# An attention and MLP kernel: the first MLP layer of tiles 2 to 8 as seven products of quarter matrices, with sums of weights kept in DRAM

## The chip, the cores and the metric

The kernel runs on one core of a Trainium2 chip. The metric is the device time of one execution in microseconds (us). Beside three plain runs there is one profiled execution, from which all durations of single instructions come.

The engines of a core work at the same time and each takes its instructions in the order of the program. TensorE (PE) multiplies matrices; the profile shows its weight loads apart, as PEld. VectorE (DVE) and ScalarE (ACT) do elementwise work. GpSimd (POOL) takes maxima across partitions. SyncE (SP) starts the transfers between DRAM and the on-chip memory. PE writes its sums into PSUM, eight banks of 128 partitions by 512 floats.

## What is computed

The reference is linear attention with random features, followed by a layer norm and a two-layer MLP with a residual:

```
phi(x)  = exp(h - max(h)) / sqrt(m),   h = x @ omega.T - |x|^2 / 2
attn    = (phi(q) @ (phi(k).T @ v)) / (phi(q) @ sum(phi(k)) + 1e-6)
xn      = (x - mean) / sqrt(var + 1e-6) * g_ln       # x is attn, heads side by side
out     = x + max(xn @ w_ch1, 0) @ w_ch2
```

There are 8 batches of 576 tokens, so 4608 tokens, 8 heads of 64, a width of 512 and a hidden width of 2048. All data are float32.

## The kernel before, in words

The tokens are cut into nine tiles of 512 (t = 0 to 8). For the MLP the hidden width is cut into 16 blocks of 128 (f = 0 to 15). The first layer (`mm1`) makes one block of the hidden layer for one tile: over the four pieces k of the width it multiplies a 128x128 piece of w1 by 512 tokens of the transposed, normalised input `xnT`. Each number is split in a high and a low part in the format fp32r, and three products replace one: high by high, low weights by high, high weights by low. So a block is 12 matmuls of 512 columns into one PSUM bank. `relu` then makes the hidden block: ACT writes the high part (L816), DVE the low part (L818). The second layer (`mm2`) multiplies the four token pieces of the hidden block by a block of w2, again 12 matmuls of 512 columns, into four banks that collect over all f. After the last f, `result` adds x (L849) and sends the tile out. `gen_mlp` puts `mm1` of a block ahead of `mm2` of the block before it, so that PE always has a second-layer block to do while the hidden block is made. All these matmuls are issued by one helper, `rounded`, and so have one line, L786.

The banks are shared out by hand: two for attention and transposes (`b_at`), two for the first layer (`b_h`), four for the second (`b_acc`).

The weights come in as 64-bit numbers and are turned into floats and split on chip (`gen_w`, L343 to L387), mainly on DVE, during tile 0 and into tile 1. All weights then stay on chip: a tile of 512 KB for each of the 16 blocks of w1 and of w2, high and low part side by side.

Attention for later tiles runs between the MLP's products: projections of keys (L514) and queries, exponentials on ACT (L451, L617), maxima of the queries on POOL (L611) which DVE subtracts (L614), sums over keys (L483), the products of queries with them (L681), division and layer norm on DVE. `gen_xnT` normalises (L757), PE transposes (L771), ACT copies the high part (L775), DVE makes the low part (L777).

The order on all engines is made when the program is built. A planner (`Plan`) runs all parts as small generators that ask for a place in memory, wait for a named event, or ask for an engine and a length. It keeps a simulated clock for each engine and always issues the part that can start first and has the lowest rank. The MLP has the highest rank number and so fills what attention leaves of PE; evacuations such as `relu` have rank MOST_URGENT. The lengths that the planner uses are written in the code, for example 0.225 us for one matmul of 512 columns, and the order is fixed by them: on the chip each engine keeps that order, whatever the real lengths are.

Of the kernel before, what the change touches and what calls it, by code (L numbers as in the profile page):

```python
# [12 lines left out]
F32 = mybir.dt.float32  # L13
# [9 lines left out]
P = 128  # L23
# [167 lines left out]
def favor_ffn(ctx, tc, kT, kTr, vF, vR, qT, qD, omT, gT, w1, w2, out):  # L191
# [17 lines left out]
    ps = ctx.enter_context(tc.tile_pool(name="ps", bufs=1, space=PSUM))  # L209
    plan = Plan()  # L210
# [54 lines left out]
    banks = names("b", 8)  # L265
    b_at, b_h, b_acc = banks[0:2], banks[2:4], banks[4:8]
# [71 lines left out]
    def gen_w(n, f):  # L338
# [35 lines left out]
        w = wparts[n, f] = tile_of(tag, [P, 2, DM], F32R)  # L374
        if n == 1:
            g = g_sb[:, f % NK : f % NK + 1]
            scaled(eng, w[:, 0], f32(t), g)
            yield dve(DM)
            nc.vector.scalar_tensor_tensor(  # L379
                out=w[:, 1], in0=f32(t), scalar=g, in1=f32(w[:, 0]), op0=ALU.mult, op1=ALU.subtract  # L380
            )
        else:
            copy(eng, w[:, 0], f32(t))
            yield dve(DM)
            nc.vector.tensor_tensor(out=w[:, 1], in0=f32(t), in1=f32(w[:, 0]), op=ALU.subtract)  # L385
        free(wt, w_turn, load_turn)
        done(("w", n, f))  # L387

# [358 lines left out]
    def gen_xnT():  # L747
        for c in range(NC):
            t, i = divmod(c, TC)
# [8 lines left out]
            done(("xn", c))  # L758
            if i == 0:
                t_t = yield "get", n_xnT  # L760
                xnTs[t] = t_t, tile_of(t_t, [P, 2, NK, T], F32R)
            plan.add(plan.cur.rank, gen_xnT1(t, i, xn, t_n, xn_turn))

# [27 lines left out]
    def mm1(t, f):  # L791
        for k in range(NK):
            yield wait("w", 1, f // NK * NK + k)
        for i in range(TC):
            yield wait("xnT", t, i)
        if not mlp_on:
            mlp_on.append(True)
        t_x, xnT = xnTs[t]
        t_b = yield "get", b_h
        ph = bank(t_b)  # L800
        for k in range(NK):
            yield us(PE, 3 * 0.225)
            w = wparts[1, f // NK * NK + k]
            cs = slice(f % NK * P, (f % NK + 1) * P)
            rounded(ph, w[:, 0, cs], xnT[:, 0, k], start=(k == 0), stop=False)
            rounded(ph, w[:, 1, cs], xnT[:, 0, k], start=False, stop=False)
            rounded(ph, w[:, 0, cs], xnT[:, 1, k], start=False, stop=(k == NK - 1))
        if f == NF - 1:
            free(t_x)
        plan.add(MOST_URGENT, relu(t, f, t_b, ph))  # L810
# [13 lines left out]

    accs = {}

    def mm2(t, f):
        yield wait("w", 2, f)
        yield wait("hid", t, f)
        t_h, hl = hid[t, f]  # L830
# [12 lines left out]
        free(t_h)  # L843

# [20 lines left out]
    def gen_mlp():  # L865
        last = None
        for t in range(NT):
            for f in range(NF):
                if f == 0 and last:
                    yield from mm2(*last)  # L870
                    last = None
# [16 lines left out]
    for f in range(NF):  # L888
        plan.add(RW + RS * (2 * f - 7 if f >= NK else f - NK), gen_w(1, f))
        plan.add(RW + RS * 2 * f, gen_w(2, f))  # L890
    plan.add(RK, gen_keys())
# [17 lines left out]
LATE = 1.0  # L909
WARM, COLD = 0.0, 5.0  # L910
# [47 lines left out]
```

## Time and profile before

| what | value |
| --- | --- |
| median of three runs | 1005.11 us (1004.85 to 1005.9) |
| profiled execution | 1004.26 us |
| its span, first to last instruction | 1002.5 us |
| granted TensorE clock over the span | 1.00 |
| PE busy | 994.9 us (99%) |
| weight loads (PEld) | 814.1 us (81%) |
| DVE busy | 500.5 us (50%) |
| ACT busy | 342.4 us (34%) |
| POOL busy | 136.7 us (14%) |
| read from DRAM, written | 52.64 MB, 9.44 MB |

How to read the profile. A row of a group has the line in the kernel, the engine, the operation, what it writes and reads (`out<-in`, numbers of buffers left out), the shape, the count, the busy time, the mean length of one in nanoseconds, and the idle time of the engine ahead of them with what ended it. A row of the timeline has the start, the length of a run of like instructions, and what they are. Matmuls are pipelined: a matmul's record reaches past the start of the next one, so the time that one costs is read from start to start, not from its length. The last addition of x (L849) of each tile begins at 168.8, 293.1, 408.8, 515.6, 626.6, 725.5, 824.4, 914.7 and 998.8 us. The lengths of the tiles differ because attention work is done between the MLP's products of the earlier ones.

### The profile page before, as it was taken

The page shows a single profiled execution, that of the slowest core. Times are in us where ns is not written, and L with a number is a line of the kernel's source. Part 1 is how long each engine was busy: PE and PEld are TensorE (multiplying, and loading weights), DVE is VectorE, ACT ScalarE, POOL GpSimd, SP SyncE. Part 2 cuts the span into 40 slices and gives each one's busy share as a digit, 9 for nine tenths or more (in the row PEclk, how much of TensorE's full clock was granted, in tenths as well). Part 3 has the DMA queues.
Part 4 walks back from the last instruction along what each step waited for, and adds up shares of the span by engine and source line. Part 5 has one row for each costly group of instructions (what it writes and reads, how often), then busy time and mean ns, then how long its engine had stood idle before and what let it go on. Part 6 is the DMA issues. An engine that isn't in the chain of part 4 may idle for free.

```text
span 1002.5 us, 16490 instructions
## 1 busy us (share of the span) xinstructions
PE 994.9 (99%) x6794; PEld 814.1 (81%) x6794; DVE 500.5 (50%) x1054; ACT 342.4 (34%) x785; POOL 136.7 (14%) x80
## 2 busy tenths in 40 slices
PE   9999999999999999999999999999999999999998
PEld 7887787788778788887888788888888888888887
DVE  6999997375357631673157423751374134113112
ACT  7587755235334520353125321331132111111100
POOL 6000633023001300140005000220032000000000
PEclk9999999999999999999999999999999999999999
DMA  9534332222132100320032100300030010001001
GB/s 355 205 148 176 110 96 84 76 74 65 43 117 77 40 12 1 129 84 1 1 127 65 43 1 11 117 1 1 26 101 1 1 43 1 0 1 43 1 1 43
DMA packets 29740, 63.16 MB, mean 63 GB/s; under 512 B 3424, under 2 KB 3552, under 8 KB 29664
## 3 DMA queue, kind: packets, MB, share of 16 engines
q1 hardware_dynamic: 29664, 62.09, 18.2%
q8 instruction: 54, 0.88, 0.4%
q14 instruction: 22, 0.18, 0.1%
HBM read 52.64 MB, written 9.44 MB: 62 GB/s over the span
## 4 chain that ended last, share of the span: by engine, by line
PE 88%; DVE 8%; issue 1%; DMA 1%; ACT 1%; SPq 0%; DVEq 0%; ACTq 0%
PE b L786 77%; PE b L681 3%; PE b L514 3%; PE b L483 3%; PE b L771 2%; DVE wide L368 1%; DVE w L354 1%; DVE w L379 1%; DVE mb L445 1%; DMA w<-w 1%; DVE hid L818 1%; DVE wide L614 1%; DMA w<-vF 1%; DVE w L385 0%; DVE x L849 0%
## 5 line engine op out<-in xcount | busy, mean ns | idle before, releaser
L786 PE MATMUL b<-w,hid 128*128 128x512 f32 x1728 | 430.1, 391 | 0.0
L786 PE MATMUL b<-xnT,w 128*128 128x512 f32 x1728 | 426.6, 390 | 0.1
L786 PEld LDWEIGHTS b<-xnT,w 128*128 128x128 f32 x1728 | 320.6, 188 | 64.9 <-issue 0.7
L786 PEld LDWEIGHTS b<-w,hid 128*128 128x128 f32 x1728 | 319.2, 188 | 63.6 <-issue 0.7
L818 DVE SCALAR_TENSOR_TENSOR hid<-b,hid 128x512 fp32r<-128x512 f32 x144 | 99.5, 691 | 376.2 <-ACT hid L816 375.8
L816 ACT ACTIVATE hid<-b 128x512 fp32r<-128x512 f32 x144 | 86.6, 601 | 449.4 <-PE b L786 448.9
L611 POOL PARTITION_ALL_REDUCE wide<-wide x72 | 135.6, 1921 | 627.1 <-ACT wide L230 538.5
L451 ACT ACTIVATE kp<-b,mb 128x128 f32<-128x128 f32 x272 | 74.4, 387 | 60.1 <-DVE mb L445 59.9
L614 DVE TENSOR_TENSOR wide<-wide,wide 128x512 f32<-128x512 f32 x72 | 65.6, 916 | 10.3 <-POOL wide L611 9.8
L445 DVE TENSOR_REDUCE mb<-b 128x4 f32<-128x512 f32 x72 | 46.7, 684 | 33.7 <-PE b L514 33.7
L617 ACT ACTIVATE wide<-wide 128x512 f32<-128x512 f32 x72 | 45.3, 635 | 48.5 <-DVE wide L614 47.8
L681 PEld LDWEIGHTS b<-kv,wide 128*64 128x64 f32 (+1 forms) x1088 | 40.5, 140 | 11.6 <-issue 8.6
L582 DVE TENSOR_TENSOR wide<-wide,wide 64x512 fp32r<-64x512 f32 x56 | 44.7, 804 | 8.3 <-ACT wide L580 6.9
L230 ACT COPY wide<-b 128x512 f32<-128x512 f32 x60 | 34.1, 591 | 35.5 <-PE b L786 28.6
L681 PE MATMUL b<-kv,wide 128*64 128x65 f32 (+1 forms) x1088 | 45.1, 227 | 0.0
L483 PEld LDWEIGHTS b<-v,kp 128*64 128x64 f32 (+2 forms) x1120 | 34.0, 138 | 13.5 <-issue 9.5
L483 PE MATMUL b<-v,kp 128*64 128x65 f32 (+2 forms) x1120 | 39.5, 226 | 0.7 <-DVE xnT L777 0.7
L514 PEld LDWEIGHTS b<-om,wide 64*128 64x128 f32 x512 | 31.1, 187 | 11.2 <-issue 7.8
L499 DVE TENSOR_TENSOR kv<-b,kv 128x260 f32<-128x260 f32 x56 | 23.2, 425 | 30.3 <-PE b L483 29.6
L514 PE MATMUL b<-om,wide 64*128 64x128 f32 x512 | 37.2, 285 | 0.0
L580 ACT CAST wide<-wide 128x512 fp32r<-128x512 f32 x56 | 33.4, 624 | 0.0
L696 DVE TENSOR_TENSOR x<-b,st 128x256 f32<-128x256 f32 x72 | 28.5, 418 | 0.4
(62 smaller groups left out, 511.1 us busy)
## 6 DMA issues: line engine op xcount, KB each, us to landing
w<-w SPq DMA_DIRECT2D x32, 512.0 KB, 7.5
wide<-qD SPq DMA_DIRECT2D x56, 256.0 KB, 2.8
out<-x SPq DMA_DIRECT2D x36, 256.0 KB, 2.0
v<-vF SPq DMA_DIRECT2D x28, 260.0 KB, 3.5
wide<-kT SPq DMA_DIRECT2D x28, 256.0 KB, 3.1
wide<-qT SPq DMA_DIRECT2D x8, 256.0 KB, 4.4
w<-vF SPq DMA_DIRECT2D x4, 260.0 KB, 4.7
v<-vR SPq DMA_DIRECT2D x4, 260.0 KB, 3.4
```

Of the source, the lines that this page charges most:

```text
L445: nc.vector.tensor_reduce(out=mb[:, 4 * s : 4 * s + 4], in_=pk, axis=AX.X, op=ALU.max, negate=True)
L451: nc.scalar.activation(out=kp[:, j], in_=pk[:, i], func=AF.Exp, scale=1.0, bias=mb[:, j : j + 1])
L483: nc.tensor.matmul(pv[s, n][m, i], kp[r, slot(h), m], v[r, h], start=(n > 0 or c + i == 0), stop=(n > 0 or (c == NFULL and i == 3)),)
L514: nc.tensor.matmul(pk[h][:, p], kraw[a, p], om[a], start=True, stop=True)
L582: nc.vector.tensor_tensor(out=qs[D:P], in0=qraw[D:P], in1=f32(qs[D:P]), op=ALU.subtract)
L611: nc.gpsimd.partition_all_reduce(mx, qc, P, bass_isa.ReduceOp.max)
L614: nc.vector.tensor_tensor(out=qc, in0=qc, in1=mx, op=ALU.subtract)
L617: nc.scalar.activation(out=qc, in_=qc, func=AF.Exp)
L681: nc.tensor.matmul(pn[a:z, i], phi(blk, h, slice(cols + a, cols + z)), kvs[b][1][:, h], start=True, stop=True)
L786: nc.tensor.matmul(out.rearrange("p (c a b) -> p c a b", a=AW, b=BW), lhsT, rhs.rearrange("p (a c b) -> p c a b", a=AW, b=BW), start=start ...
L816: nc.scalar.activation(out=hl[:, 0], in_=ph, func=AF.Relu)
L818: nc.vector.scalar_tensor_tensor(out=hl[:, 1], in0=ph, scalar=0.0, in1=f32(hl[:, 0]), op0=ALU.max, op1=ALU.subtract)
```

## The change

From tile 2 on (SEVEN = 2) the first layer goes by Strassen's scheme in Winograd's form. The 16 blocks are taken as four groups g of 512 hidden columns. A group of w1 and the tile's input are each cut in four quarters: the width in two halves of 256, the hidden columns in two halves of 256, the tokens in two halves of 256. Instead of eight products of quarters there are seven. Their operands on the side of the input are the quarters B11, B21, B22 and the differences T1 = B12 - B11, T2 = B22 - T1, T3 = B22 - B12, N4 = B21 - T2. On the side of the weights they are three quarters as they are and four sums of quarters.

The sums of weights are made once, on DVE and ACT, while tiles 0 and 1 run (`gen_sides`, `halved`, `lesser`), split in high and low parts, and written to DRAM (`side`, 2 MB for each group). For each tile and group they are loaded again, 512 KB each, into one place on chip for each of the four (`gen_ring`); a place is loaded again when both steps of the group have read it. The four places are those of four w1 blocks, freed by moving one needed half elsewhere (`gen_move`).

Twelve of the 16 blocks of w2 no longer stay on chip either. They are written to DRAM when they are made (`gen_leave`, `kept`) and, from tile 2 on, loaded for each tile, two taking turns in one place (`gen_return`). The six places gained hold operands (three), the differences before they are split (two) and a working tile u (one). The other four operands take the place of `xnT`.

For each tile the operands are made thus: the two token pieces of a pair are transposed and copied whole (`gen_turned`), DVE makes the differences, and each of the seven is split by a copy (ACT or DVE) and a subtraction on DVE (`parted`). The second pair waits until the first has been split.

The first layer is now eight steps a tile, each for two hidden blocks, h of group g (`seven`). A step has seven products of 6 matmuls with 256 columns. The two banks of the first layer hold four halves x, y, v, z of 256 columns:

```
before = (t, g, h - 1) if h else (t, g - 1, 1) if g else (t - 1, NK - 1, 1)
before = before if before[0] >= SEVEN else None
yield wait("moved", g)
yield "get", ("one",)
yield from run(x, 0, plain(0, 0), "B11", True)
yield from run(y, 2, None, "T2")
plan.add(MOST_URGENT, second(t, g, h, before, x, y, u))
yield "get", ("two",)
yield from run(v, 1, None, "T1", True)
yield from run(z, 3, None, "T3")
plan.add(MOST_URGENT, fourth(t, g, h, before, v, z, u))
yield wait("u2", t, g, h)
yield from run(x, 0, plain(0, 1), "B21")
plan.add(MOST_URGENT, first(t, g, h, x, u))
yield from between()
yield wait("c22", t, g, h)
yield from run(v, 4, None, "B22")
yield from run(z, 0, plain(1, 1), "N4")
plan.add(MOST_URGENT, third(t, g, h, before, two, u))
```

`between` is one second-layer block, and another follows each step. `second` copies x to u on ACT and adds y on DVE; `fourth` adds v and z on DVE; `first` makes the half of a hidden block that x holds; `third` adds u to the second bank and makes the rest. All additions have one line, L1104; the matmuls of 256 columns have L1041, those of 512 columns L991 (L786 before), the halves of hidden blocks L1130, the additions of x L1193 (L849 before), the subtraction of the query maxima L717 (L614 before).

The core of the diff; the functions above and the loading and storing are left out:

```
         if n == 1:
+            w = wparts[n, f] = tile_of(tag, [P, 2, 2, HC], F32R)
...
+        if n == 2 and f in LENT:
+            plan.add(LEAVE, gen_leave(f, w))
...
+    def product(out, left, right, start):
+        def passes(x):
+            return x.rearrange("p (a c b) -> p c a b", b=8, c=4)
+
+        for k in range(2):
+            for l, r in ((0, 0), (1, 0), (0, 1)):
+                nc.tensor.matmul(
+                    passes(out), left(k, l), passes(right[:, r, k]), start=start and k + l + r == 0,
+                    stop=k + r == 2, skip_group_check=True,
+                )
...
+    def second(t, g, h, before, x, y, u):
+        if before:
+            yield wait("cc", *before)
+            yield wait("c22", *before)
+        yield act(HC)
+        nc.scalar.copy(out=u[:, 0], in_=x)
+        yield dve(HC)
+        add(u[:, 0], y, u[:, 0])
+        done(("u2", t, g, h))
...
     def gen_mlp():
...
         for t in range(NT):
-            for f in range(NF):
-                if f == 0 and last:
-                    yield from mm2(*last)
-                    last = None
-                yield from mm1(t, f)
-                if last:
-                    yield from mm2(*last)
-                last = t, f
-        yield from mm2(*last)
+            for f in range(NF if t < SEVEN else NF // 2):
+                if f == 0:
+                    yield from one()
+                    yield from one()
+                if t < SEVEN:
+                    yield from mm1(t, f)
+                    yield from one()
+                    last.append((t, f))
+                else:
+                    g, h = divmod(f, 2)
+                    yield from seven(t, g, h, one)
+                    yield from one()
+                    last += [(t, NK * g + h), (t, NK * g + 2 + h)]
...
+SEVEN, HC = 2, DM // 2
+SHARED, HOSTS = (4, 5, 6, 7, 2, 3), 8
+LENT = (*SHARED, *(f + HOSTS for f in SHARED))
+LEAVE, RSIDE = 24, 24
```

At the seam between two tiles PE has three second-layer blocks of the old tile behind the last step's products, and the first step of a tile has none inside it.

More of the change, by code (lines that the diff above doesn't have):

```diff
@@ new lines, in halved, with lesser @@
+    def halved(g, k, n, t_h, t_s, s):
+        hi = tile_of(t_h, [P, 2, HC], F32R)
+        eng = yield "run", {ACT: 0.56, DVE: 0.34}
+        copy(eng, hi, s)
+        yield dma(P * DM)
+        nc.sync.dma_start(sides[g, 0][:, 2 * n : 2 * n + 2, 0, k], f32(hi))
+        plan.add(plan.cur.rank, lesser(g, k, n, t_s, s, hi, t_h))
+    def lesser(g, k, n, t_s, s, hi, t_h):
+        yield dve(DM)
+        nc.vector.tensor_tensor(out=s.bitcast(F32R), in0=s, in1=f32(hi), op=ALU.subtract)
+        free(t_h)
+        yield dma(P * DM)
+        nc.sync.dma_start(sides[g, 0][:, 2 * n : 2 * n + 2, 1, k], s)
+        free(t_s)
+        done(("side", g, n, k))
@@ L764, in gen_xnT1, with parted @@
+    def parted(t, name, i, x):
+        yield wait("op", t, name)
+        o = ops[t, name][1]
+        eng = yield "run", {ACT: 0.3, DVE: 0.28}
+        copy(eng, o[:, 0, :, i * P : (i + 1) * P], x)
+        yield dve(HC)
+        nc.vector.tensor_tensor(
+            out=o[:, 1, :, i * P : (i + 1) * P], in0=x, in1=f32(o[:, 0, :, i * P : (i + 1) * P]), op=ALU.subtract
+        )
+        done(("x2", t, name, i))
     def gen_xnT1(t, i, xn, t_n, xn_turn):
@@ new lines, in add, with fourth @@
+    def add(out, left, right):
+        nc.vector.tensor_tensor(out=out, in0=left, in1=right, op=ALU.add)
+    def second(t, g, h, before, x, y, u):
[4 more added lines that the diff above has]
+        nc.scalar.copy(out=u[:, 0], in_=x)
+        yield dve(HC)
+        add(u[:, 0], y, u[:, 0])
+        done(("u2", t, g, h))
+    def fourth(t, g, h, before, v, z, u):
+        if before:
+            yield wait("hid", before[0], NK * before[1] + 2 + before[2])
+        yield wait("u2", t, g, h)
+        yield dve(HC)
+        add(u[:, 3], v, u[:, 0])
+        yield dve(HC)
+        add(u[:, 3], z, u[:, 3])
+        done(("c22", t, g, h))
@@ new lines, in halves, with first @@
+    def halves(hl, cols, x):
+        yield act(x.shape[1], 1, 0.05)
+        nc.scalar.activation(out=hl[:, 0, cols], in_=x, func=AF.Relu)
+        yield dve(x.shape[1])
+        nc.vector.scalar_tensor_tensor(
+            out=hl[:, 1, cols], in0=x, scalar=0.0, in1=f32(hl[:, 0, cols]), op0=ALU.max, op1=ALU.subtract
+        )
+    def first(t, g, h, x, u):
+        f = NK * g + h
+        t_h = yield "get", n_hid
+        hl = tile_of(t_h, [P, 2, T], F32R)
+        hid[t, f] = t_h, hl
+        yield from halves(hl, slice(0, HC), x)
+        free("one")
+        yield wait("cc", t, g, h)
+        yield from halves(hl, slice(HC, T), u[:, 1])
+        done(("hid", t, f))
@@ new lines, in third @@
+    def third(t, g, h, before, two, u):
+        f = NK * g + 2 + h
+        if before:
+            yield wait("hid", before[0], NK * before[1] + before[2])
+            yield wait("hid", before[0], NK * before[1] + 2 + before[2])
+        yield dve(2 * HC)
+        add(
+            u[:, 1:3], two.rearrange("p (a b) -> p a b", b=HC),
+            u[:, 0:1].to_broadcast([P, 2, HC]),
+        )
+        free("two")
+        done(("cc", t, g, h))
+        yield wait("c22", t, g, h)
+        t_h = yield "get", n_hid
+        hl = tile_of(t_h, [P, 2, T], F32R)
+        hid[t, f] = t_h, hl
+        yield from halves(hl, slice(0, T), u[:, 2:4].rearrange("p a b -> p (a b)"))
+        done(("hid", t, f))
@@ L829, in mm2 @@
         yield wait("hid", t, f)
+        lent = f in LENT
+        if lent and t >= SEVEN:
+            yield wait("back", t, f)
         t_h, hl = hid[t, f]
@@ L843, in mm2 @@
         free(t_h)
+        if lent and t >= SEVEN - 1:
+            free(*n_w[2, f + HOSTS if t >= SEVEN and f in SHARED else f])
     def result(t, i, acc):
```

214 lines of the change are left out of this document (206 added, 8 removed).

## The prediction

> **What bounds the kernel now.** I read the page's busy rows first, then the chain that ended last, then the stages tile by tile, then single stretches of the timeline.
>
> ```profile
> span 1002.5 us, 16490 instructions
> PE 994.9 (99%) x6794; PEld 814.1 (81%) x6794; DVE 500.5 (50%) x1054; ACT 342.4 (34%) x785; POOL 136.7 (14%) x80
> PE 88%; DVE 8%; issue 1%; DMA 1%; ACT 1%; SPq 0%; DVEq 0%; ACTq 0%
> PE b L786 77%; PE b L681 3%; PE b L514 3%; PE b L483 3%; PE b L771 2%; DVE wide L368 1%; DVE w L354 1%; DVE w L379 1%; DVE mb L445 1%; DMA w<-w 1%; DVE hid L818 1%; DVE wide L614 1%; DMA w<-vF 1%; DVE w L385 0%; DVE x L849 0%
> ```
>
> TensorE sets the end, and 77% of the chain is the two MLP layers (L786). DVE is busy half the time, PE almost never waits. So a change is worth what it takes out of PE's stream, less every wait that it puts into it. The stages, cut where the last result (L849) begins, of tiles 1, 2, 5 and 8 (columns: window, length, then busy time and count of PE, PEld, DVE, ACT, POOL, the granted clock, DMA share and GB/s):
>
> ```profile
> 168.80:293.10 124.30, 124.10 (x1099) 99.58 (x1097) 63.24 (x145) 49.88 (x144) 15.02 (x8) 1.00 0.23 67
> 293.10:408.80 115.70, 114.72 (x887) 92.89 (x888) 54.77 (x119) 37.64 (x92) 14.70 (x8) 1.00 0.16 49
> 626.60:725.50 98.90, 98.90 (x546) 80.76 (x545) 42.90 (x90) 24.50 (x46) 14.81 (x8) 1.00 0.10 33
> 914.70:998.80 84.10, 84.04 (x382) 71.28 (x381) 13.78 (x22) 9.56 (x16) 0.00 (x0) 1.00 0.03 12
> ```
>
> Now the pitch of a product of 512 columns, from groups of twelve in the timeline: first two groups of tile 5, then two of tile 7.
>
> ```profile
> 703.88 2.94 PE L786 MATMUL b<-xnT,w 128*128 128x512 f32 x12
> 706.65 2.93 PE L786 MATMUL b<-w,hid 128*128 128x512 f32 x12
> ...
> 862.11 2.80 PE L786 MATMUL b<-xnT,w 128*128 128x512 f32 x12
> 864.75 2.80 PE L786 MATMUL b<-w,hid 128*128 128x512 f32 x12
> ```
>
> Start to start it is 2.77/12 = 0.2308 us in one place and 2.64/12 = 0.220 us in the other, at the same granted clock of 1.00 (the rows above). The kernel has both paces, and a stretch keeps its pace until PE is interrupted. I take their mean, 0.2255, for tiles 2 to 8.
>
> **Part 1: fewer columns streamed (gain).** Seven of nine tiles change. Each had 16 x 12 = 192 first-layer products of 512 columns; it now has 8 steps x 7 quarter products x 6 matmuls = 336 of 256 columns. Taken out: 7 x 192 x 0.2255 = 303.1 us. Put in: 2352 matmuls whose pitch no row shows, since no fp32r product of 256 columns runs today. The nearest rows are a bf16 product of 256 columns, and fp32 products of 65 columns whose 128x128 weights are the longer part:
>
> ```profile
> 37.99 4.09 PE L308 MATMUL b<-spin 128*128 128x256 bf16 x36
> 30.45 0.53 PEld L681 LDWEIGHTS b<-kv,wide 128*128 128x128 f32 x4
> L681 PEld LDWEIGHTS b<-kv,wide 128*128 128x128 f32 x64 | 8.1, 192 | 0.1
> L786 PEld LDWEIGHTS b<-xnT,w 128*128 128x128 f32 x1728 | 320.6, 188 | 64.9 <-issue 0.7 <-DVE xnT L777 0.5
> ```
>
> The bf16 row gives (4.09 - 0.27 for the last one's length)/35 = 0.109 us. In the second row four loads of 0.192 us stand within 0.53 us, so they begin (0.53 - 0.192)/3 = 0.113 us apart: a load's recorded time is not its pitch, and loads overlap each other as well as products. Stream (0.109) and load (0.113) of a 256-column product are then nearly equal. Low bound: the load's pitch, 0.112. High bound: the slow pace keeps its whole extra per product, 0.2308 - 2 x 0.109 + 0.109 = 0.122. I take 0.116, a little nearer to the load row, because both paces occur. Then 2352 x 0.116 = 272.8 us and the gain is 30.3 us; the bounds give 303.1 - 263.4 = 39.7 and 303.1 - 286.9 = 16.2 us.
>
> By the Trainium skill (TensorE: Matmul & The Clock Gate, section Back-to-back issue gap) 256 columns take 262 cycles at 2.4 GHz, 0.109 us, and 512 columns 518, 0.216 us; by that 1344 x 0.216 - 2352 x 0.109 = an estimated 34 us would be saved. The bf16 row agrees, the 512-column rows are 2 to 7% above it, so the rows decide.
>
> **Part 2: waits inside a step (loss).** The order on PE in tile 8, before: the end of a second-layer block and a whole first-layer block (w are weights, hid the hidden layer, xnT the input, b a PSUM bank):
>
> ```order
> L786 MATMUL b_8386<-w_130_1557,hid_8711 128x512 x3
> L786 MATMUL b_8754<-xnT_8272,w_120_1214 128x512 x3
> L786 MATMUL b_8754<-xnT_8272,w_130_1304 128x512 x3
> L786 MATMUL b_8754<-xnT_8272,w_140_1377 128x512 x3
> L786 MATMUL b_8754<-xnT_8272,w_150_1450 128x512 x3
> ```
>
> And in the changed kernel one step (bank b_3454 holds the halves x and y, b_3455 the halves v and z; weights w_50, w_10, w_90, w_130 are the loaded sums):
>
> ```order
> L1041 MATMUL b_3454<-w_40_2540,w_80_970 128x4x8x8 x6
> L1041 MATMUL b_3454<-w_50_2641,w_50_10484 128x4x8x8 x6
> L1041 MATMUL b_3455<-w_60_2738,w_10_10493 128x4x8x8 x6
> L1041 MATMUL b_3455<-xnT_3341,w_90_10502 128x4x8x8 x6
> L1041 MATMUL b_3454<-xnT_3341,w_100_1191 128x4x8x8 x3
> L1041 MATMUL b_3454<-xnT_3341,w_110_1273 128x4x8x8 x3
> L991 MATMUL b_10330<-w_130_10207,hid_10517 128x512 x3
> ```
>
> Before, a first-layer block filled one bank and nothing read it until a second-layer block had run. Now the fifth product adds into x, which ACT must first have copied and DVE must have added to y; only the third and fourth products, 12 x 0.116 = 1.39 us, lie between. What the chain y -> ACT -> DVE -> PE costs, from these rows:
>
> ```profile
> 731.55 0.86 PE L786 MATMUL b<-w,hid 128*128 128x512 f32 x3
> 731.75 0.60 ACT L816 ACTIVATE hid<-b 128x512 fp32r<-128x512 f32 x1 [3.44 <-PE b L786]
> 732.38 0.69 DVE L818 SCALAR_TENSOR_TENSOR hid<-b,hid 128x512 fp32r<-128x512 f32 x1 [0.71 <-ACT hid L816]
> ...
> L230 ACT COPY kv<-b 128x260 f32<-128x260 f32 x16 | 5.6, 376 | 9.9 <-PE b L483 9.7
> L499 DVE TENSOR_TENSOR kv<-b,kv 128x260 f32<-128x260 f32 x56 | 23.2, 425 | 30.3 <-PE b L483 29.6
> L614 DVE TENSOR_TENSOR wide<-wide,wide 128x512 f32<-128x512 f32 x72 | 65.6, 916 | 10.3 <-POOL wide L611 9.8
> ```
>
> ACT starts 0.20 us after the stream has gone on to the next product, and DVE 0.03 us after ACT. So the chain is 0.20 + 0.38 + 0.03 + 0.43 + 0.03 = 1.07 us, 0.32 us inside its cover, if ACT and DVE are free. When DVE is in the middle of something else the cover is gone. The order on DVE in tile 5, before:
>
> ```order
> L818 SCALAR_TENSOR_TENSOR hid_6511<-b_6481,hid_6511 128x512
> L716 BN_AGGR st_5492<-st_5492 128x2
> L582 TENSOR_TENSOR wide_6496<-wide_6487,wide_6496 64x512
> L727 TENSOR_SCALAR st_5492<-st_5492 128x2
> L614 TENSOR_TENSOR wide_6505<-wide_6505,wide_6513 128x512
> ```
>
> and after (L1104 are a step's additions, L717 is what was L614, the query maxima subtracted):
>
> ```order
> L685 TENSOR_TENSOR wide_7794<-wide_7785,wide_7794 64x512
> L1104 TENSOR_TENSOR w_70_3456<-b_3454,w_70_3456 128x256
> L717 TENSOR_TENSOR wide_7813<-wide_7813,wide_7823 128x512
> L1104 TENSOR_TENSOR w_70_3456<-b_3455,w_70_3456 128x256
> L717 TENSOR_TENSOR wide_7820<-wide_7820,wide_7831 128x512
> L1104 TENSOR_TENSOR w_70_3456<-b_3455,w_70_3456 128x256
> ```
>
> Attention's work now stands between additions that PE waits for. DVE's load per tile: a step has 3 additions of 256 (0.42), one of 512 (0.69), two half relus (0.43) and a whole one (0.69), 3.5 us, 28 per tile against 16 x 0.69 = 11 before; the operands add 8 differences and 14 low parts of 0.42 less the four old low parts of 0.69, some 6.5 us. That is +24 us: about 79 of 110 us in tile 2, 67 of 94 in tile 5, 31 of 80 in tile 8. Between 0 (the chain always inside its cover) and 0.92 us a step (always one L614 in front) I take 0.2 us for the 40 steps of tiles 2 to 6, where a mean DVE instruction is 500.5/1054 = 0.47 us and meets a 0.32 us cover, and 0.05 for the other 16: 9 us. The waits on the second pair of banks have the second-layer block of 2.7 us as cover, and cost nothing until DVE is 1.5 us late.
>
> **Part 3: the seams (loss).** The seven operands of a tile (quarters of xn and their differences) replace those of the tile before when its last step has read them; 28 pieces are copied (ACT or DVE) and reduced (DVE) while three second-layer blocks, 8.1 us, run. The first operand needs a copy and a difference of the last one, transposes, an ACT copy, a copy and a difference, about 4 us by the durations above; T2 and T1 follow 2 to 3 us later. I take 0.5 us for each of six seams, 3 us (0 to 10). Into tile 2 only two blocks (5.4 us) cover the same, with four operands left to do first: 3 us (0 to 6).
>
> **Part 4: sums of weights and DRAM.** Making the sums is 8 x (4 of 0.73, 4 of 0.42) = 37 us of DVE and ACT, in tile 1: DVE goes from 63 to about 100 of 124 us. PE has other work there; 1 us (0 to 5). Transfers: each changed tile loads 16 sums and 12 second-layer blocks of 512 KB, 14.7 MB, some 155 GB/s on top of the 12 to 49 in the rows above.
>
> ```profile
> GB/s 355 205 148 176 110 96 84 76 74 65 43 117 77 40 12 1 129 84 1 1 127 65 43 1 11 117 1 1 26 101 1 1 43 1 0 1 43 1 1 43
> w<-w SPq DMA_DIRECT2D x32, 512.0 KB, 7.5
> ```
>
> The first slice shows 355 GB/s, so the sum fits. A ring place is free from its product in one step to the same product in the next: 42 x 0.116 + 24 x 0.2255 = 10.3 us, and a block landed in 7.5 us at the busiest time. So I cost it at nothing; SP issues in order, and if it falls behind, PE waits at every change of group.
>
> **The sum.** -30.3 + 9 + 3 + 3 + 1 = -14.3 us. The profiled run took 1004.26 us (1.8 us around its span); the median of the three runs is 1005.11. So 1005.1 - 14.3, say 990.8 us.
>
> **The rivals.**
> Waits stay small and the pitch is the load's (chance 0.20): -39.7 + 7 or so, about 972 us. For it: PE is busy 99% today though hundreds of attention products wait for DVE and ACT. Against it: those had slack, and the slow pace occurs.
> DVE takes PE's place in tiles 2 to 6 (0.17): each of 40 steps waits for one L614-like instruction, 40 x 0.92 = 37, 0.8 for the others, 7 for the seams: -30.3 + 45 = +15, 1020 us. It decides from (30.3 - 8)/40 = 0.56 us a step. For it: the DVE order above. Against it: DVE is below 75%.
> Loads bind (0.03): each load takes its recorded 0.188 us and the products wait for it, 2352 x 0.188 - 303.1 = +139, 1144 us; it decides from a pitch of 303.1/2352 = 0.129. Against it stands the row of four loads in 0.53 us. Two places of the Trainium skill speak for it. TensorE: Matmul & The Clock Gate, section The mechanism, lets a load overlap products in flight only when it goes to another row group, and here all use all rows. Perfetto Trace Analysis, section Identifying the Most-Contended Engine, judges PE's headroom by the busy share of loads, 81% here, which 1008 more would fill. The trace disagrees with both as far as it shows: 0.188 us loads lie inside 0.220 us products.
> The ring is late (0.06): a kept block goes ahead of a sum on SP's queue and each of 21 changes of group inside a tile waits 2 us, +42 - 14, about 1033 us.
>
> **Chances.** The forecast has 0.54 (some 980 to 1002). About 0.2% (2 us) is what a measurement here can tell from no change. Faster by more: 0.54 + 0.20, less 0.02 for the forecast's upper edge: 0.72. Within 0.2%: that 0.02 and 0.04 of the DVE case: 0.06. Slower: 0.13 + 0.06 + 0.03 = 0.22. Range: 969 (gain of 39.7 with some 4 us of waits) to 1012 (gain of 16.2 with 0.3 us a step and the seams at their bounds, or the milder half of the DVE case); it leaves out loads, ring and the worse DVE cases, some 0.16, and 0.04 below.
>
> **What would show it.** Right: twelve L1041 matmuls start to start 1.35 to 1.47 us; tile 8, where attention is gone, shorter by 192 x 0.220 - 336 x 0.116 = 3.3 us, or a little more at 0.112; PE's waits named L1041 <- DVE, 5 to 15 us in all, mostly in tiles 2 to 6; DVE near 79 us in tile 2. Wrong: a pitch over 0.129; waits over 25 us; PE waiting for DMA at L1041; tile 1 longer than 124 us by more than 5.

## The result and the profile after

| what | before | after |
| --- | --- | --- |
| median, us (four runs each, on one chip) | 1005.5 (1004.85 to 1006.01) | 993.97 (993.41 to 995.0) |
| profiled execution, us | 1004.26 | 995.0 |
| its span, us | 1002.5 | 993.1 |
| span less busy time of PE, us | 7.6 | 17.4 |

The ratio is 0.9887 (95% interval 0.987 to 0.9904): faster by 1.1%, 11.5 us by the medians and 9.4 us by the two spans. 14.3 us were forecast.

The head of the page after, its chain, and the groups of the MLP's products and of the new additions:

```profile
span 993.1 us, 19831 instructions
PE 975.7 (98%) x7816; PEld 839.3 (85%) x7816; DVE 680.4 (69%) x1530; ACT 417.2 (42%) x1009; POOL 139.7 (14%) x80
...
PE 85%; DVE 9%; DMA 3%; ACT 1%; issue 1%; SPq 0%; DVEq 0%
...
L991 PE MATMUL b<-w,hid 128*128 128x512 f32 x1728 | 434.3, 394 | 0.0
L1041 PE MATMUL b<-xnT,w 128*128 128x256 f32 x1344 | 178.6, 279 | 2.4 <-DVE w L1104 2.3
L1041 PE MATMUL b<-w,w 128*128 128x256 f32 x1008 | 129.0, 279 | 0.5 <-DVE w L964 0.5
L1041 PEld LDWEIGHTS b<-xnT,w 128*128 128x128 f32 x1344 | 167.9, 188 | 8.8 <-DVE w L1104 3.3
L1104 DVE TENSOR_TENSOR w<-b,w 128x256 f32<-128x256 f32 x224 | 109.4, 489 | 49.7 <-PE b L1041 35.4
```

TensorE still sets the end, with 19 us less of work, but 10 us more in which it does nothing. The new additions (L1104) hold it up for only 2.3 us, as the idle columns of the L1041 groups say. The same stages as in the prediction, tiles 1, 2, 5 and 8:

```profile
165.50:293.90 128.40, 124.73 (x1033) 99.11 (x1029) 92.56 (x202) 55.62 (x141) 25.46 (x14) 1.00 0.43 137
293.90:412.00 118.10, 117.15 (x1155) 100.86 (x1153) 86.00 (x199) 54.34 (x154) 14.62 (x8) 1.00 0.55 178
624.10:721.00 96.90, 94.91 (x690) 84.79 (x689) 62.17 (x147) 34.03 (x77) 15.73 (x8) 0.98 0.57 185
905.90:989.50 83.60, 83.13 (x526) 74.32 (x524) 31.38 (x64) 14.23 (x32) 0.00 (x0) 1.00 0.42 135
```

The nine tiles went from 168.8, 124.3, 115.7, 106.8, 111.0, 98.9, 98.9, 90.3 and 84.1 us to 165.5, 128.4, 118.1, 104.6, 107.5, 96.9, 96.7, 88.2 and 83.6. Tile 1, which keeps the old scheme, lost 4 us, and tile 2, which has the new one, lost 2.4. The counts on PE (x) say part of why: tile 1 has 66 instructions fewer than before (1099 to 1033), and tile 2 has 268 more (887 to 1155) where the scheme adds only 336 - 192 = 144. Attention's products have moved from the first tiles into tile 2. Tile 1 is longer with less to do because PE idles there for 3.7 us (128.40 - 124.73), where it idled for 0.2 before. Tiles 3 to 7 gained 2.0 to 3.5 us each, and tile 8, in which nothing but the MLP is left, 0.5 where 3.3 were forecast. One step of it in the timeline:

```profile
931.85 2.25 PE L1041 MATMUL b<-w,w 128*128 128x256 f32 x18
933.94 1.52 PE L1041 MATMUL b<-xnT,w 128*128 128x256 f32 x12
935.30 2.92 PE L991 MATMUL b<-w,hid 128*128 128x512 f32 x12
938.05 1.57 PE L1041 MATMUL b<-xnT,w 128*128 128x256 f32 x12
939.47 2.92 PE L991 MATMUL b<-w,hid 128*128 128x512 f32 x12
942.22 2.25 PE L1041 MATMUL b<-w,w 128*128 128x256 f32 x18
```

From start to start the 42 products of a step take 2.09 + 1.36 + 1.42 = 4.87 us, 0.116 each. Two old blocks took 24 x 0.220 = 5.28 here. That is 0.41 us gained in each of eight steps, the 3.3 us. But a block of the second layer now takes 2.75 us where it took 2.64: 0.2292 us a product instead of 0.220. Sixteen blocks give 1.8 us back, and nothing in the second layer was changed. Of the 1.0 us that is still missing in tile 8, 0.4 is idle time of PE (83.60 - 83.13, with next to none before); the rest is not assigned. Last, what PE waited for (in all, times, longest):

```profile
PE b L917 <- ACT wide L231: 4.0, 2, 2.0
PE b L1041 <- DVE w L1104: 2.3, 3, 1.2
PE b L917 <- DVE wide L862: 1.4, 2, 1.0
...
PE b L586 <- DVE xnT L982: 1.2, 1, 1.2
PE b L991 <- ACT xnT L980: 1.1, 1, 1.1
```

The largest waits are at the transposes of the normalised input (L917, L771 before), which stand in the order behind evacuations that came late. The waits at attention's products (L586) and at the first layer of the old scheme (L991) are in tile 1.

Counted over all distances from start to start on PE, the two profiles differ as follows in tiles 2 to 8 (a pitch for each kind of product, and what lies above it as waits and interruptions):

| part | forecast, us | measured, us |
| --- | --- | --- |
| first layer: 302.9 to 270.3 (mean pitch 0.1151) | -30.3 | -32.6 |
| other products of 512 columns: 0.2254 to 0.2283 each | 0 | +3.9 |
| waits and interruptions | +15 (9 + 3 + 3) | +13.9 |
| attention's work come over from tiles 0 and 1 | 0 | +5.1 |
| tiles 0 and 1 together | +1 | +0.8 |

These add up to -8.9; 0.5 of the 9.4 us stays unassigned.

### The profile page after: what moved, and what is told of

The parts are those of the page before. It is cut to its first block, busy times and chain, and to the rows that moved or that the text cites. A ratio compares the mean times of both kernels' runs of the same rounds, so it can differ in the third digit from the quotient of the medians.

```text
span 993.1 us, 19831 instructions
## 1 busy us (share of the span) xinstructions
PE 975.7 (98%) x7816; PEld 839.3 (85%) x7816; DVE 680.4 (69%) x1530; ACT 417.2 (42%) x1009; POOL 139.7 (14%) x80
## 4 chain that ended last, share of the span: by engine, by line
PE 85%; DVE 9%; DMA 3%; ACT 1%; issue 1%; SPq 0%; DVEq 0%
PE b L991 47%; PE b L1041 26%; PE b L784 3%; PE b L586 3%; PE b L617 3%; DMA wide<-qD 2%; DVE wide L685 1%; PE b L917 1%; DVE wide L717 1%; DMA w<-w 1%; DVE x L1193 1%; DVE wide L862 1%; DMA w<-kT 1%; PE b L657 0%; DVE xnT L982 0%
## 5 line engine op out<-in xcount | busy, mean ns | idle before, releaser
L991 PE MATMUL b<-w,hid 128*128 128x512 f32 x1728 | 434.3, 394 | 0.0
L991 PEld LDWEIGHTS b<-w,hid 128*128 128x128 f32 x1728 | 314.2, 188 | 62.2 <-issue 0.7
L1041 PE MATMUL b<-xnT,w 128*128 128x256 f32 x1344 | 178.6, 279 | 2.4 <-DVE w L1104 2.3
L1041 PEld LDWEIGHTS b<-xnT,w 128*128 128x128 f32 x1344 | 167.9, 188 | 8.8 <-DVE w L1104 3.3
L1104 DVE TENSOR_TENSOR w<-b,w 128x256 f32<-128x256 f32 x224 | 109.4, 489 | 49.7 <-PE b L1041 35.4
L1041 PE MATMUL b<-w,w 128*128 128x256 f32 x1008 | 129.0, 279 | 0.5 <-DVE w L964 0.5
L1041 PEld LDWEIGHTS b<-w,w 128*128 128x128 f32 x1008 | 124.4, 188 | 5.7 <-DVE w L964 0.7
L1130 DVE SCALAR_TENSOR_TENSOR hid<-w,hid 128x256 fp32r<-128x256 f32 x112 | 67.9, 606 | 74.7 <-ACT hid L1128 73.9
L1128 ACT ACTIVATE hid<-w 128x256 fp32r<-128x256 f32 x112 | 58.4, 528 | 135.3 <-PE b L991 69.0
L991 PE MATMUL b<-xnT,w 128*128 128x512 f32 x384 | 98.0, 395 | 1.3 <-ACT xnT L980 1.1
L1130 DVE SCALAR_TENSOR_TENSOR hid<-b,hid 128x256 fp32r<-128x256 f32 x56 | 23.7, 424 | 91.0 <-ACT hid L1128 90.9
L991 PEld LDWEIGHTS b<-xnT,w 128*128 128x128 f32 x384 | 70.5, 188 | 18.2 <-ACT xnT L980 1.5
L1128 ACT ACTIVATE hid<-b 128x256 fp32r<-128x256 f32 x56 | 21.6, 386 | 147.0 <-PE b L991 134.9
L717 DVE TENSOR_TENSOR wide<-wide,wide 128x512 f32<-128x512 f32 x72 | 65.0, 904 | 5.5 <-POOL wide L714 5.1
L231 ACT COPY wide<-b 128x512 f32<-128x512 f32 x67 | 38.5, 591 | 17.9 <-PE b L991 11.3
```

The costliest lines, as they stand in the source:

```text
L717: nc.vector.tensor_tensor(out=qc, in0=qc, in1=mx, op=ALU.subtract)
L991: nc.tensor.matmul(out.rearrange("p (c a b) -> p c a b", a=AW, b=BW), lhsT, rhs.rearrange("p (a c b) -> p c a b", a=AW, b=BW), start=start ...
L1041: nc.tensor.matmul(passes(out), left(k, l), passes(right[:, r, k]), start=start and k + l + r == 0, stop=k + r == 2, skip_group_check=True,)
L1104: nc.vector.tensor_tensor(out=out, in0=left, in1=right, op=ALU.add)
L1128: nc.scalar.activation(out=hl[:, 0, cols], in_=x, func=AF.Relu)
L1130: nc.vector.scalar_tensor_tensor(out=hl[:, 1, cols], in0=x, scalar=0.0, in1=f32(hl[:, 0, cols]), op0=ALU.max, op1=ALU.subtract)
```

## The experiments

Each was timed against the kernel before, on the same chip. My theory after the result: the products of 256 columns bring the slow pace of the second layer, the sums of weights displace attention's work, and the transfers cost nothing. The rivals: the transfers (178 GB/s for 49 in tile 2, 135 for 12 in tile 8) slow PE's stream; and the waits come from an order made with wrong lengths.

**halves_before.** The kernel before, each first-layer product issued as two of 256 columns. No scheme, no transfers, no additions.

```
-            rounded(ph, w[:, 0, cs], xnT[:, 0, k], start=(k == 0), stop=False)
...
+            for l, r in ((0, 0), (1, 0), (0, 1)):
+                for j in range(2):
+                    nc.tensor.matmul(
+                        ph[:, j * QB : (j + 1) * QB].rearrange("p (c a b) -> p c a b", a=AW, b=BW), w[:, l, cs],
+                        xnT[:, r, k].rearrange("p (a c b) -> p c a b", a=AW, b=BW)[:, 2 * j : 2 * j + 2],
...
```

> The kernel before, with each first-layer matmul of 512 columns issued as two of 256 columns with the same weights; nothing else changes, and no transfer is added. If matmuls of 256 columns themselves set the slow pace of the second layer: second-layer groups of twelve take 2.75 us (0.229 each) in all tiles, tiles 7 and 8 too (0.220 there before); the halves take 0.113 to 0.118, and the time is about 1020 us (1728 x (2 x 0.1145 - 0.2248) = +7 and 1728 x 0.0047 = +8). If instead the transfers of the changed kernel set that pace: the second layer keeps its two paces, 0.220 in tiles 7 and 8, and the time is about 1012 us.

Measured: 1032.67 us, ratio 1.0268 (1.0252 to 1.0283). Its timeline in tile 8:

```profile
937.28 5.87 PE L807 MATMUL b<-xnT,w 128*128 128x256 f32 x48
942.99 2.93 PE L786 MATMUL b<-w,hid 128*128 128x512 f32 x12
945.76 1.46 PE L807 MATMUL b<-xnT,w 128*128 128x256 f32 x11
```

A product of 256 columns takes 5.71/48 = 0.119 us, and the block behind it 2.77/12 = 0.231, in a tile where the same block had 0.220. So the slow pace needs neither transfers nor the scheme: products of 256 columns around a block bring it (straight, below, narrows this to the way they read). The loss was well above what I had thought, as these halves never come to the 0.1133 us seen in the changed kernel. They too read in runs of eight, 32 apart, but across all 512 tokens; why they are slower is open.

**no_reload.** The changed kernel with sums and kept blocks loaded for tile 2 alone; later tiles multiply with whatever lies in the places then, and the work on the engines is the same.

```
-                yield dma(2 * P * DM)
-                r = tile_of(tag, [P, 2, 2, HC], F32R)
-                nc.sync.dma_start(f32(r), sides[g, 0][:, n])
+                if t == SEVEN:
+                    yield dma(2 * P * DM)
+                    r = tile_of(tag, [P, 2, 2, HC], F32R)
+                    nc.sync.dma_start(f32(r), sides[g, 0][:, n])
```

> The changed kernel, with sums of weights and second-layer weights loaded for tile 2 only; tiles 3 to 8 reuse what lies on chip, so the loading (some 88 MB, and its places on SP's queue) is left out. If the waits at attention's products in tiles 5 and 6 (about 2.2 us each, with what follows) come from query loads standing behind reloads on SP's queue: they go, the time falls by 6 to 9 us to about 986, and the second layer stays at 0.229. If the traffic also slows PE's own reads: the second layer returns to a mean of 0.2255 and the time to about 981. If the order on DVE and ACT makes the waits: at most 2 us less, 992.

Measured: 989.74 us, ratio 0.9844 (0.9828 to 0.9861), so 4.2 us under the changed kernel. Tile 5, and the longest of PE's waits:

```profile
623.10:717.40 94.30, 93.34 (x690) 83.53 (x689) 62.14 (x147) 34.12 (x77) 15.97 (x8) 1.00 0.11 34
PE b L919 <- ACT wide L231: 3.8, 4, 1.0
```

With 34 GB/s in place of 185 the second layer still runs at 0.228 us, so transfers are not what slows it. Tiles 5 and 6 are 2.6 and 2.5 us shorter and the other tiles stay within 0.8. The transpose (L919, L917 in the changed kernel) waits 1.0 us at most where it waited 2.0, and part of the 4.2 us is a matter of the clock. In the changed kernel's profile, where that wait is (the transposes, then a window behind the restart):

```profile
646.78 0.41 PE L991 MATMUL b<-wide,om_lo 128*128 128x512 f32 x1
649.18 0.63 PE L917 MATMUL b<-ident,wide 128*128 128x128 f32 x4 [2.00 <-ACT wide L231]
...
650.60:654.00 3.40, 3.40 (x13) 2.81 (x12) 3.37 (x9) 2.01 (x4) 0.87 (x1) 0.50 0.56 154
```

PE has next to nothing for some 2 us, and 1.4 us after it restarts the granted clock is 0.50 for 3.4 us. The other wait of 2.0 us, in tile 6, is followed by no such spell. Nor does one occur in tile 5 of read_steps (below), whose transfers run as in the changed kernel:

```profile
621.60:716.20 94.60, 93.38 (x690) 83.57 (x689) 62.18 (x147) 34.09 (x79) 15.77 (x8) 1.00 0.58 190
```

Tile 5 takes 94.6 us there, where its longest wait is 1.2 us, 94.3 here and 96.9 in the changed kernel. So the gain in tile 5 is nearly all that of the shorter wait and of the missing spell (an estimated 1.7 us, half of 3.4), and the spell can be missing with the transfers running. Why the evacuation (L231) comes later with the transfers running can be followed back in the changed kernel's profile:

```profile
631.29 2.99 SPq L488 DMA_DIRECT2D w<-side  x3
634.33 1.36 SPq L678 DMA_DIRECT2D wide<-qD  x2
...
641.70 0.62 ACT L683 CAST wide<-wide 128x512 fp32r<-128x512 f32 x1 [1.29 <-DMA wide<-qD]
```

A load of queries (qD) is issued behind three loads of sums and lands 7.3 us later; ACT waits for it, and the chain that leads to the late L231 begins there. In all ACT waits 10.7 us for such loads, 5.2 in no_reload.

**straight.** The operands lie on chip so that a product reads its tokens in runs of eight, 32 apart ("in steps"), and the changed kernel's product writes PSUM in the same steps. Here both go straight on.

```
-                    passes(out), left(k, l), passes(right[:, r, k]), start=start and k + l + r == 0,
+                    out, left(k, l), right[:, r, k], start=start and k + l + r == 0,
```

> The changed kernel, with the matmuls of 256 columns reading and writing their columns one after another, without the steps of 32. If the pitch is that of the weight load: 0.113 settled as now, and the time within 2 us of 994. If the way through memory sets the pitch: more or less than 0.113 settled; at 0.119 settled it would be +14 us, 1008.

Measured: 994.97 us, ratio 0.9901 (0.9882 to 0.9919): 1.0 us more than the changed kernel, which is within the spread of either. But the two paces went opposite ways: 256 columns at 0.1191 (2352 x 0.004 = +9.4 us), the second layer at 0.2225 in tile 8 and at 0.2249 as the mean of tiles 2 to 8, for 0.2283 (some -5 us). The rest of what makes up for the slower products was not assigned.

**read_steps and write_steps** part the two: only the reading in steps, and only the writing (in both, tokens come out in another order).

```
-                    passes(out), left(k, l), passes(right[:, r, k]), start=start and k + l + r == 0,
+                    out, left(k, l), passes(right[:, r, k]), start=start and k + l + r == 0,
```

```
-                    passes(out), left(k, l), passes(right[:, r, k]), start=start and k + l + r == 0,
+                    passes(out), left(k, l), right[:, r, k], start=start and k + l + r == 0,
```

> The changed kernel; its matmuls of 256 columns still read the operand in steps of 32 columns, but write PSUM straight on. The tokens of the hidden blocks then stand in another order, so this part of the output is not the reference's. If the way of reading sets the paces: 256 columns settle at 0.113, the second layer stays at 0.229, time 994. If the way of writing sets them: 256 columns settle at 0.120 and the second layer comes near 0.222, as with both straight on, about 995.

> The same the other way round: the matmuls of 256 columns read straight on and write PSUM in steps of 32 (tokens of the hidden blocks in another order). If reading sets the paces: 0.120 settled and the second layer near 0.222, about 995. If writing sets them: 0.113 and 0.229, about 994. If each sets one of the two: 0.113 with 0.222 in one of the two kernels, which would be worth 1344 x 0.007 = 9 us there, about 985.

Measured: 993.87 us (0.9892, 0.9872 to 0.9911) and 997.08 us (0.9918, 0.9898 to 0.9938). The timelines of tile 8, read_steps first:

```profile
931.20 1.52 PE L1041 MATMUL b<-xnT,w 128*128 128x256 f32 x12
932.56 2.92 PE L991 MATMUL b<-w,hid 128*128 128x512 f32 x12
935.32 1.57 PE L1041 MATMUL b<-xnT,w 128*128 128x256 f32 x12
```

```profile
927.70 1.60 PE L1041 MATMUL b<-xnT,w 128*128 128x256 f32 x12
929.14 2.83 PE L991 MATMUL b<-w,hid 128*128 128x512 f32 x12
931.81 1.59 PE L1041 MATMUL b<-xnT,w 128*128 128x256 f32 x12
```

Reading in steps gives 1.36/12 = 0.1133 and 2.76/12 = 0.230, like the changed kernel; reading straight on gives 1.44/12 = 0.120 and 2.67/12 = 0.2225. How PSUM is written makes no difference to the two paces. So the way in which a product reads its operand sets its own pace and that of the block behind it, in opposite directions. It is not the length of the product that does it: the halves of halves_before took 0.119, nearly as long as straight ones, but read in steps, and the block behind them was slow.

**lengths.** The changed kernel with the planner's lengths taken from the trace (a dozen such lines):

```
-    def dve(n, k=1, c=0.065):
+    def dve(n, k=1, c=0.155):
...
-        eng = yield "run", {ACT: 0.56, DVE: 0.34}
+        eng = yield "run", {ACT: 0.63, DVE: 0.57}
```

> The changed kernel, with the planner's lengths for DVE, ACT and the hops between engines taken from the trace (DVE 256 columns 0.424 for 0.334, 512 columns 0.69 for 0.60, a hop behind DVE or ACT 0.05 for 0.2). If the waits come from an order made with wrong lengths: PE's waits in tiles 2 to 8 fall from about 14 us over the level of before to under 7, and the time to 986 to 988. If they come from SP's queue: within 3 us of 994.

Measured: 1000.24 us, ratio 0.9946 (0.9931 to 0.9961), slower than the changed kernel by 6.3. Tiles 5 and 6 are shorter (93.8 and 94.2), tiles 2 and 3 longer (125.2 and 108.8), and a new wait leads the list:

```profile
PE b L979 <- DVE wide L865: 3.3, 1, 3.3
```

So better lengths alone did not remove the waits: another order moves them, and this one put the longest at the end of tile 0.

**from_tile_3.** The new scheme from tile 3 on (`SEVEN = 3`); tile 2 keeps the old one.

> The changed kernel with the scheme from the fourth tile on (six tiles for seven). If each changed tile gains what tiles 3 to 7 gained (2 to 3.5 us) and the sums of weights cost what tiles 0 to 2 lost together (+3.2 us) because DVE is full there: tile 2 is back at 115.7, the sums have three tiles to be made in, and the time is 989 to 992. If tile 2's loss is attention work that only moves on: tile 3 shows it instead, and the time is 994 to 997.

Measured: 995.47 us, ratio 0.9909 (0.9892 to 0.9925). Tile 2:

```profile
291.00:413.50 122.50, 122.50 (x1033) 97.86 (x1030) 63.41 (x146) 48.66 (x131) 15.80 (x8) 1.00 0.29 95
```

PE is busy without a break and tile 2 still takes 122.5 us, 6.8 more than in the kernel before, with 1033 - 887 = 146 more instructions of attention. Neither expectation came true: the displaced work stays in tile 2 though the scheme starts a tile later, so it is not the scheme that brings it there. Without the scheme tile 2 takes 4.4 us more than with it.

**pool_sums.** Sums of weights and differences of operands on GpSimd, to free DVE.

```
-            nc.vector.tensor_tensor(out=f32(x), in0=f32(w[:, :, 0]), in1=f32(w[:, :, 1]), op=ALU.add)
+            nc.gpsimd.tensor_tensor(out=f32(x), in0=f32(w[:, :, 0]), in1=f32(w[:, :, 1]), op=ALU.add)
```

> The changed kernel with the sums of weights and the differences of operands made by GpSimd instead of DVE (8 x 6 and 7 x 8 instructions, some 60 us off DVE). If attention's products wait because DVE is full: waits of PE over the level of before fall from 14 us to 7 or less, the time to 986 to 989. If they wait because of SP's queue: within 2 us of 994. If GpSimd is slow at it (over 2 us for 512 columns) or slows DVE: later sums, 996 or more.

Measured: 1149.43 us, ratio 1.144 (1.1423 to 1.1457): a miss. A group of GpSimd, the first of PE's waits and one of DVE's:

```profile
L432 POOL TENSOR_TENSOR wide<-w 128x512 f32<-128x512 f32 x16 | 26.4, 1660 | 67.0 <-DVE w L382 25.2 <-ACT w L237 18.6 <-DVE wide L370 7.6
PE b L1041 <- DVE w L1104: 68.7, 8, 14.3
DVE wide L717 <- POOL wide L714: 110.5, 22, 14.4
```

An addition of 512 columns takes 1660 ns there, a difference of 256 takes 905 and 830, and they stand in one queue with the maxima of 1.9 us. That queue then holds up what DVE needs (the last row: the query maxima, one of them for 14.4 us), and DVE the step. It shows what the step's additions cost when something stands in front: 68.7 us. In the changed kernel it is 2.3. The granted clock fell too, to 0.94 over the span, so the 155 us lost are not waits alone.

**no_sums.** The changed kernel without making the sums: parts of the weights are written in their place, so the transfers stay and the additions, copies and their four buffers go. The first layer of tiles 2 to 8 thus multiplies with parts instead of sums.

```
-        tags = yield "get", n_big, 4
...
+            w = wparts[1, NK * g + k + 2 * n]
+            for half in range(2):
+                yield dma(P * DM)
+                nc.sync.dma_start(sides[g, 0][:, 2 * n : 2 * n + 2, half, k], f32(w[:, :, half]))
```

> The changed kernel without making the sums of weights: parts of the weights as they are go to DRAM in their place, by as many bytes, and are loaded as before (so the first layer of the changed tiles is not the reference's). 48 additions, 16 copies and 16 low parts, some 45 us of DVE and ACT, and their four buffers are gone from tiles 0 to 2. If these cost what tiles 0 to 2 lost (+3.2 us together, and more since 5 us of PE's work moved from tile 1 to tile 2): 987 to 990. If that loss is that of the seam and of transfers: 993 to 994.

Measured: 989.13 us, ratio 0.9837 (0.9822 to 0.9852), 4.8 us under the changed kernel. Tiles 1 and 2:

```profile
167.30:295.30 128.00, 127.24 (x1140) 102.26 (x1141) 69.66 (x163) 53.04 (x145) 15.80 (x8) 1.00 0.37 119
295.30:408.30 113.00, 110.77 (x1042) 96.40 (x1041) 78.17 (x183) 50.87 (x138) 15.29 (x8) 1.00 0.55 178
```

Tile 1 has its attention work back (1140 instructions on PE, 1033 with the sums) and tile 2 is rid of it (1042, 1155 with the sums). Tiles 0 to 2 end at 408.3 us instead of 412.0. So the sums cost 3.7 us there: PE idles in tile 1 for 0.8 us without them (128.00 - 127.24) and 3.7 with them, and the work that it did not get done comes in tile 2. In the profile the rest lies mainly in tile 5, 2.1 us shorter without a half-clock spell, and in tile 6, 1.1 us shorter.

**last_straight and last_three.** If the reading just ahead of a block sets its pace, it is enough that the last products ahead of each block read straight on, and the rest keep 0.1133. In last_straight these are all six products of B21 and of N4, in last_three the last three of each.

```
-        def passes(x):
+        def passes(x, k):
+            if last and k >= 1:
+                return x
...
-            product(out, left, ops[t, name][1], start)
+            product(out, left, ops[t, name][1], start, name in ("B21", "N4"))
```

> The changed kernel; in the two products that stand just ahead of a second-layer block (B21 and N4) the matmuls of 256 columns read and write straight on, the other five in steps of 32. Theory: in steps of 32 a product of 256 columns is as short as its weight load (0.113), loads run without slack, and the second layer that follows keeps the slow pace; read straight on (0.120) loads have slack and the second layer falls to 0.220 after two products. Then the second layer is at 0.222 to 0.224 where B21 or N4 is right ahead of it, twelve straight matmuls a step cost 12 x 0.005 = 0.06 and 24 second-layer matmuls gain 24 x 0.007 = 0.17: -0.11 us a step, -6 us in all, about 988. Rival, the pace hangs on the mean of all products: second layer about 0.227, time 994 to 996.

> The same, but only the last three matmuls of B21 and N4 read straight on. If three loads with slack are enough: second layer 0.222 to 0.224 and about 986 to 987. If more are needed: second layer still 0.229 and 994 to 995.

Measured: 988.74 us (0.9836, 0.982 to 0.9853) and 985.96 us (0.9807, 0.9788 to 0.9826). The second is the fastest of all versions, 8.0 us under the changed kernel, with the whole of the work done. Not all of the 8.0 us comes from the pace: the granted clock was 0.998 over the span in all four executions of the changed kernel and in two of this one (988.4 and 987.1 us), and 1.000 in the other two (984.8 and 983.8). At 0.998 the gain is some 6 us, and the two versions are within about 1 us of each other. Tile 8 of last_three:

```profile
926.59 2.20 PE L1043 MATMUL b<-w,w 128*128 128x256 f32 x18
928.63 1.54 PE L1043 MATMUL b<-xnT,w 128*128 128x256 f32 x12
930.01 2.82 PE L991 MATMUL b<-w,hid 128*128 128x512 f32 x12
932.67 1.54 PE L1043 MATMUL b<-xnT,w 128*128 128x256 f32 x12
```

The 18 take 0.1133 us each, the 12 with three straight ones 1.38/12 = 0.115, and the block 2.66/12 = 0.2217, where the changed kernel has 0.116, 0.1133 to 0.118 and 0.2292. So three are enough here. The reason given with last_straight, that loads have slack behind products of 0.120, does not fit halves_before, where products of 0.119 leave the slow pace.

**before_straight.** Does the same help the kernel before? There the last product of each block of twelve reads straight on (L792).

```
-            rounded(ph, w[:, 0, cs], xnT[:, 1, k], start=False, stop=(k == NK - 1))
+            (straight if k == NK - 1 else rounded)(ph, w[:, 0, cs], xnT[:, 1, k], start=False, stop=(k == NK - 1))
...
-            rounded(accs[i], hl[:, 1, cs], w[:, 0], start=False, stop=(f == NF - 1))
+            (straight if i == TC - 1 else rounded)(accs[i], hl[:, 1, cs], w[:, 0], start=False, stop=(f == NF - 1))
```

> The kernel before, in which the last of the twelve matmuls of every block of the first and the second layer (288 of 3456) reads its operand straight on and writes its product in the order that this asks for; the result stays the same. Theory (the way in which the moving operand is read sets the pace of the matmuls behind it): the blocks of twelve in tiles 5 and 6 go from 0.2305 us to about 0.222 us a matmul, and the time from 1005.5 to 992 to 995 us. Rival (the fast pace came back in the version with the last three products read straight only as it was in the kernel before, whose pace is already the best): the pace stays at 0.2305 there, the straight reads cost 288 x 0.015 to 0.02 us, and the time is 1009 to 1011 us.

Measured: 1012.18 us, ratio 1.0066 (1.0053 to 1.008). The time is 1.2 us above the rival's range, but the timeline is neither's. In tile 5:

```profile
692.45 2.58 PE L786 MATMUL b<-xnT,w 128*128 128x512 f32 x11
694.87 0.39 PE L792 MATMUL b<-xnT,w 128*128 128x512 f32 x1
695.10 2.70 PE L786 MATMUL b<-w,hid 128*128 128x512 f32 x11
697.64 0.40 PE L792 MATMUL b<-w,hid 128*128 128x512 f32 x1
697.88 2.58 PE L786 MATMUL b<-xnT,w 128*128 128x512 f32 x11
```

Eleven products take 2.42 us, 0.220 each, then one reads straight on, then eleven take 2.54, 0.231 each, then again 2.42. Each straight product turns the pace over, from slow to fast and from fast to slow, and so it goes in tile 8 too. Tiles 5 and 6, slow before, gain 1.2 us each; tiles 7 and 8, fast before, lose 2.4 each. "Straight reading ahead of a block makes it fast" is therefore too simple a rule: what a change of reading does depends on the pace that was there.

## Why the prediction was right, and where its steps were not

**Part 1 held.** The pitch was taken as 0.116 between the load's 0.112 and the slow pace's 0.122; it is 0.1151 over the seven tiles and 0.116 in the rows of tile 8. The gain was 32.6 us for 30.3. Both bounds are there: the 256-column products settle at 0.1133, close to the load's pitch, and run at 0.116 to 0.124 for eight products behind a change of kind. Loads do not bind at their recorded 0.188 us: in the changed kernel loads recorded at 188 ns (L1041 PEld, above) belong to products 0.1133 us apart. A line of the Trainium skill (TensorE: Matmul & The Clock Gate, section The mechanism) lets a load overlap products in flight only when it goes to another row group, though the section names a background weight buffer too; no row here bears the first out.

**What Part 1 left out** is that the new products change the pace of the others. It said that a stretch keeps its pace until PE is interrupted and took the mean, 0.2255. In fact a block of 512 columns between products of 256 that read in steps runs at about 0.229 each time, and where before it had 0.220, as in tile 8, more than half of that tile's gain goes back. The runs read_steps and write_steps show that this comes from the reading of the products ahead, and halves_before that it needs nothing else of the scheme; no_reload rules out the transfers. It cost 3.9 us in all. By what mechanism the reading sets the pace is open.

**Part 2 named the right chain and mis-sized it.** Waits at L1104 are 2.3 us, not 9. DVE's load was about as forecast (86 us in tile 2 for 79, 62 in tile 5 for 67, 31 in tile 8 for 31), but the unlucky order, L717 in front of an addition, made PE wait in only three of the 56 steps, 1.2 us at most. The rival in which DVE takes PE's place needed 0.56 us in each of 40 steps; pool_sums shows that it exists when an engine ahead of DVE is slow enough.

**The total of Parts 2 and 3 held by luck.** Waits and interruptions came to 13.9 us for 15, but not where they were put: the seams, forecast at 6 us, show a wait for operands (L964) of 0.5. Of the waits by name the largest lie at the transposes of the normalised input (5.4 us, 1.2 before). The clock belongs here too: one of the two waits of 2 us is followed by 3.4 us at half clock, an estimated 1.7 us lost in tile 5.

**Part 4 failed on both counts.** Sums of weights were put at 1 us, "PE has other work there". In fact PE idles in tile 1 for 3.7 us, and attention's work goes from tile 1 into tile 2: no_sums gives 4.8 us, 3.7 of it in tiles 0 to 2. Transfers were put at nothing unless PE waits for a sum at a change of group. They cost by another way: the loads of queries stand behind them on SP's queue, and ACT waits. no_reload gives 4.2, of it an estimated 1.7 for the half-clock spell, which read_steps does without though it has the same transfers. How the two overlap was not tried together. Nothing waited at L1041 for DMA in the changed kernel's list of waits, and the rival of the late ring fell.

So the forecast of 990.8 was 3.2 us too low: some 2 us more gain and 6 less wait in the steps, against 4 us of pace, 5 of displaced work and the waits elsewhere. The upper end of the range, 1012, was lower than its own terms give: 1005.1 - 16.2 + 0.3 x 40 + 10 + 6 + 1 = 1017.9.

## What to carry to other kernels

Fewer columns streamed are worth their pitch, but look at the pitch of the neighbours as well: a new kind of product can change the pace of products that nobody touched, and the tile where everything else is gone shows it. Work "beside" the bound engine is not free when it displaces other work that must be done on that engine later; compare the counts of each stage, not only its waits. Before deciding on a layout, time a product with its operand read straight on and in steps, and the products behind it.

## What the runs showed of the hardware

- A stream of products of 512 columns, read in runs of eight, has two paces at full clock, 0.220 and 0.231 us. A single product that reads straight on turned one into the other, both ways. In tile 8, three, six or more straight products of 256 columns ahead of a block left 0.220 (0.2217 to 0.2225 with the first products of the block), none left 0.230. What keeps the state is open.
- In the changed kernel a product of 256 columns took 0.1133 us read in steps and 0.120 read straight on; how it was written to PSUM did not matter. The halves of halves_before, read in steps across 512 tokens, took 0.119.
- After some 2 us without PE work the granted clock fell to 0.50 for 3.4 us, beginning 1.4 us after the restart; another wait of the same length brought no fall. The Trainium skill (TensorE: Matmul & The Clock Gate, section What's actually happening) gives windows of about 3.4 us; the length agrees, but the idle time that was enough here is shorter.
